# Spectral filter + GEGLU kernel: leftover columns in four groups of 32 partitions, twiddle tables split between VectorE and GpSimd, column loop written out

## The chip, the core and the metric

The kernel runs on one core of one Trainium2 chip. The metric is device time in microseconds (us) of one execution. TensorE is called PE (its weight loads PEld), VectorE DVE, ScalarE ACT, GpSimd POOL; SP is the engine whose instruction stream issues nearly all DMAs of this kernel, in program order.

## The reference

One transformer-like block on x of shape (1, 2048, 576), bf16: a spectral filter over the normalised x, then a GEGLU feed-forward network, each with a residual.

```python
def _A_ref(x, w_r, w_i):            # x: (1, 2048, 576); w_r, w_i: (2048, 289)
    X = rfft2(x.astype(float32), axes=(-2, -1))
    X = X * (w_r + 1j * w_i)
    return irfft2(X, s=(2048, 576), axes=(-2, -1)).astype(bfloat16)

def _B_ref(x, w_gate, w_up, w_down):   # w_gate, w_up: (576, 4608); w_down: (4608, 576)
    return (gelu(x @ w_gate) * (x @ w_up)) @ w_down

h   = x + _A_ref(layernorm(x), w_r, w_i)
out = h + _B_ref(layernorm(h), w_gate, w_up, w_down)
```

## The kernel before

The 2048 rows are split as 128 partitions times 16 (`h`), and the length-2048 Fourier transform as 16 (rows h, with a 128-wide table `F16`) and 128 (columns, with the twiddle tables). All is one program with `manual_schedule`: each engine executes its instructions in the order in which the program issues them, and so does each engine's DMA queue; engines meet through semaphores, which come from the data dependences and from the rotation of buffers. PSUM has four buffers of two banks (`two`), which all stages take in turn.

The stages, in order:

1. **Row stage** (about 4 to 21 us). x is loaded in six chunks. DVE (`sd`) and ACT (`ln_act`) make means and variances, POOL the reciprocal deviations (`ln_rstd`) and minus twice the means (`minus_means`). `norms(lo, hi)`: DVE scales the table `F16` by rstd of a row h into `FR`, and `row16(h)` multiplies on PE the columns of that row with it into PSUM (`f2t`), for the columns 0 to 255 and 288 to 543 of the 576. `evict` copies two rows at a time to `Bt[:, 0:4]` on ACT. The columns left over, 256 to 287 and 544 to 575, are the "leftovers" or "rests": `rests(h)` does four rows, each with four matmuls (`row16_rest`, L351) into 64 partitions for either half, and `evict4` copies them to `Bt[:, 4]`.
2. **Tables.** `DT` holds the sines and cosines of the column transform (`phases`, `col_sin`, `mirror`); `DF` is a copy of its third part for the leftovers' partitions, zero elsewhere. `DQ` is `DT` in another layout, made by small DMAs (`load_dq`). `TF` holds nine twiddles, each with minus sine, cosine and sine (slots 0, 1, 2); their angles are made on DVE (`angle_a` multiply-add, `angle_b` modulo 2048, `angle_s` shift, `angle_c` magnitude), the sines on ACT (`sine`, `cosine`), the negation on DVE (`minus_sine`). `first` are twiddles 0 and 1, `rest` are 2 to 8. `TI` is `TF` transposed by DMA from SP (`turn_tf`).
3. **Filter.** `WR` and `WI` hold rows 0 to 16 of the filter per partition: rows 0 to 8 come straight from HBM, rows 9 to 16 in reversed partition order, gathered by POOL into `wm` (`gather`) and copied from there by SP (L504). POOL then halves the first and the last column of all rows (L508).
4. **Column loop.** For the eight k of `order = [1, ..., 7, 0]`: `f2(c)` for c = k and k + 8 multiplies `Bt` with `DT` and `DF` on PE into `pq_ps` (six matmuls each, L550), `f2_out` copies to `pq`; `f3(k, half)` applies the twiddle (L567, L568; copies g and hs on ACT); `sum_of` combines the halves on DVE; `wmul` multiplies with the filter on DVE (`times`, L618, with rows k and 17 - k of WR, then of WI; `parts`, L623 and L624; Zt, L638 and L639 or, for k = 0, L641 and L642); `i3(k, s)` goes back with `TI` on PE (L658; for k = 0 L682), ACT copies to `EO`. Steps of neighbouring k are interleaved, `wmul` one and `i3` three iterations behind `f2`. `inv_cols` (L709) and `add_rows` then finish the inverse transform.
5. **FFN** (from about 65 us to the end). Layernorm, `gate` (L978, gate and up), the product with w_down (L1021, L1040), and the output.

Of the kernel before, what the change touches and what calls it, by code (L numbers as in the profile page):

```python
# [20 lines left out]
P = 128  # L21
# [21 lines left out]
def kernel_body(  # L43
# [45 lines left out]
    neg = keep.tile([P, 2], FP32, name="neg")  # L89
    for i in range(2):  # L90
        V.memset(neg[:, i : i + 1], -2.0 + i)
    mneg = keep.tile([P, 2, H], BF16, name="mneg")
# [18 lines left out]
    DF = keep.tile([P, 2, 2, JH], BF16, name="DF")  # L111
# [28 lines left out]
    def minus_means(lo, hi):  # L140
        sh = [P, 2, hi - lo]
        G.tensor_tensor(
            mneg[:, :, lo:hi],
            mv[:, lo:hi, 0].unsqueeze(1).to_broadcast(sh),
            neg[:].unsqueeze(2).to_broadcast(sh),
            ALU.mult,
        )
# [19 lines left out]
    for t, w in ((WR, A_w_r), (WI, A_w_i)):  # L167
        nc.sync.dma_start(t[:, 0:9, 0:J], w.rearrange("(p r) j -> p r j", r=H)[:, 0:9, :])
# [19 lines left out]
    V.memset(DF[:], 0.0)  # L188
# [18 lines left out]
    iota(iD[64:128, 2:3], [[0, 1]], 2 * P + 64 + 192, 1)  # L207
# [50 lines left out]
    first, rest = slice(0, 2), slice(2, 9)  # L258
# [15 lines left out]
    def angle_c(sl):  # L274
        drop_sign(ab[:, sl], ab[:, sl])

# [36 lines left out]
    def fill(dst, n):  # L313

        for _ in range(n):
            T.matmul(dst, lhsT=ident[:], rhs=h_sb[:, 0, 0:512], start=True, stop=True)

    def row16(h):
# [6 lines left out]
        for t in range(2):  # L325
            for n, d0 in ((0, t * P), (1, DH + t * P)):
# [9 lines left out]
                lhsT=mneg[:, 0, h : h + 1].to_broadcast([P, P]),  # L336
# [5 lines left out]
    def rests(h):  # L342
        ps_f["f4", h] = two("f4")
        for i in range(4):
            row16_rest(h + i)

    def row16_rest(h):
        o = (h % 4) * P
        for mean in (False, True):
            for p0, d0 in ((0, 256), (64, 512)):  # L350
                T.matmul(  # L351
                    ps_f["f4", h - h % 4][p0 : p0 + 64, 0, o : o + P],
                    lhsT=mneg[:, 1, h : h + 1].to_broadcast([P, 64]) if mean else h_sb[:, h, d0 : d0 + 64],
                    rhs=FR[:, h, 0, :],
                    start=not mean,
                    stop=mean,
                )
# [8 lines left out]
    def evict4(h):  # L366
        (V.tensor_copy if h >= 8 else A.copy)(
            Bt[:, 4, :].rearrange("p (c h l) -> p h c l", c=16, h=16)[:, h : h + 4, :, :],
            ps_f["f4", h][:, 0].rearrange("p (h c l) -> p h c l", h=4, c=16),
        )  # L370
# [71 lines left out]
    sd(2, 4)  # L442
# [19 lines left out]
    rests(0)  # L462
# [5 lines left out]
    rests(4)  # L468
# [4 lines left out]
    evict(0, 2)  # L473
    evict4(0)
    evict(4, 6)
    evict4(4)
# [6 lines left out]
    rests(8)  # L483
# [8 lines left out]
    rests(12)  # L492
# [5 lines left out]
    mirror(0)  # L498
    evict4(8)
    V.tensor_copy(DF[0:32], D3[0:32])  # L500
    V.tensor_copy(DF[96:128], D3[96:128])
    evict4(12)
    for w, t in ((WR, wm[0]), (WI, wm[1])):
        nc.sync.dma_start(w[:, 9 : H + 1, 0:J], t[:].rearrange("p (r j) -> p r j", r=8))  # L504
    angle_a(rest)
    angle_b(rest)
# [5 lines left out]
    def load_dq(r):  # L512
        for w in range(1 - r, NW):
            j0, j1 = w * JW, (w + 1) * JW
            for lo, hi in ((j0, min(j1, (j0 // P + 1) * P)), ((j0 // P + 1) * P, j1)):
                if lo < hi:
# [3 lines left out]
                    )  # L520

# [21 lines left out]
    def f2(c):  # L543
        ps = two("pq_ps")
        col = slice(slot[c] * P, (slot[c] + 1) * P)
        steps = [(par, t) for par in range(2) for t in (par, par + 2, 4)]
        if c == order[0]:
            steps.sort(key=lambda s: s[1] == 4)
        for par, t in steps:
            T.matmul(  # L550
                ps[:, par, 0:JP],
                lhsT=Bt[:, t, col],
                rhs=DT[:, t // 2, par] if t < 4 else DF[:, par],
                start=(t == par),
                stop=(t == 4),
            )
        pq[c] = wk.tile([P, 2, JP], BF16, name="pq", tag="pq", bufs=6)
        pq_ps[c] = ps
# [541 lines left out]
```

## Time and profile before

| | |
|---|---|
| Median of three timed runs | 494.39 us (494.04 to 494.93) |
| Profiled execution, its own time | 494.6 us |
| its span | 492.8 us, 12868 instructions |
| PE busy | 484.7 us (98%), PEld 338.9 (69%) |
| DVE busy | 223.4 us (45%) |
| ACT busy | 158.2 us (32%) |
| POOL busy | 29.5 us (6%) |
| Granted TensorE clock | 9 tenths or more in all 40 slices |

A line of the timeline has start and duration in us, engine, line, operation, output and inputs with their shapes, the number of instructions merged into it, and in brackets how long the engine had been idle and what ended the idle time. "SPq" is the issue of a DMA by SP; its data land later. A line of the table by stretches has the stretch, its length, then busy time and number of instructions of PE, PEld, DVE, ACT and POOL, the granted clock, the DMA share and GB/s. A line of the chain in order of time has start, duration, engine, tile and line. The duration of a DVE, ACT or PE instruction includes a tail that overlaps the next one; the cost of one in a row of them is the distance from start to start.

### The profile page before, as it was taken

What the parts mean: (1) busy time and instruction counts of PE and PEld (TensorE: products, weight loads), DVE (VectorE), ACT (ScalarE), POOL (GpSimd) and SP (SyncE); (2) the same over time, 40 slices, a digit from 0 to 9 for tenths busy, and PEclk for the clock granted to TensorE, in tenths of its full rate; (3) what the DMA queues carried; (4) which work ended last, traced back from release to release, by engine and by line L of the source; (5) the groups of instructions that cost most, each with busy time, mean ns of one, the idle gap of its engine ahead of it and who ended that gap; (6) DMA issues with size and microseconds to landing.
All of it is one profiled execution on the core that took longest, in us unless ns stands there. A gap on an engine that the chain in (4) does not pass through costs nothing.

```text
span 492.8 us, 12868 instructions
## 1 busy us (share of the span) xinstructions
PE 484.7 (98%) x5762; PEld 338.9 (69%) x5762; DVE 223.4 (45%) x457; ACT 158.2 (32%) x280; POOL 29.5 (6%) x84
## 2 busy tenths in 40 slices
PE   6999999999999999999999999999999999999997
PEld 3777789875589955555699755555799655555995
DVE  8999774798622177333311345333121333333111
ACT  8899863322210022332200132332110232232000
POOL 8500010011100011000000000000000000000000
PEclk9999999999999999999999999999999999999999
DMA  8838979769970049966720089876600377760000
GB/s 278 234 74 184 246 115 240 165 128 212 223 161 3 3 118 195 192 145 147 152 65 1 37 170 199 174 145 147 143 3 3 92 158 155 150 146 1 14 13 25
DMA packets 89582, 62.35 MB, mean 127 GB/s; under 512 B 23222, under 2 KB 88118, under 8 KB 89526
## 3 DMA queue, kind: packets, MB, share of 16 engines
q1 hardware_dynamic: 89238, 60.34, 57.5%
q0 software_dynamic: 288, 1.18, 0.7%
q8 instruction: 45, 0.74, 0.7%
q14 instruction: 11, 0.09, 0.1%
HBM read 52.65 MB, written 2.36 MB: 112 GB/s over the span
## 4 chain that ended last, share of the span: by engine, by line
PE 95%; ACT 2%; POOL 1%; DMA 1%; issue 0%; DVE 0%; ACTq 0%; POOLq 0%
PE gu L978 57%; PE acc L1021 27%; PE pq_ps L550 2%; PE cs_ps L709 2%; PE acc L1040 2%; PE eo_ps L658 2%; ACT junk L128 1%; PE y_ps L848 1%; PE gh_ps L568 1%; PE gh_ps L567 1%; DMA h_sb<-in_A_x_dram 1%; POOL rstd L138 1%; ACT Bt L361 0%; POOL wm_r L397 0%; PE eo_ps L682 0%
## 5 line engine op out<-in xcount | busy, mean ns | idle before, releaser
L978 PE MATMUL gu<-Bt,wgu 64*128 64x512 bf16 (+1 forms) x2646 | 270.6, 363 | 0.0
L978 PEld LDWEIGHTS <-wgu 64*128 64x128 bf16 x2646 | 151.5, 94 | 115.6 <-issue 0.3
L987 DVE TENSOR_TENSOR P_sb<-g_sb,gu 128x512 bf16<-128x512 f32 (+1 forms) x156 | 100.4, 645 | 140.3 <-ACT g_sb L986 140.3
L986 ACT ACTIVATE g_sb<-gu 128x512 f32<-128x512 f32 (+1 forms) x156 | 88.0, 564 | 193.5 <-PE gu L978 193.5
L1021 PEld LDWEIGHTS <-P_sb 64*128 64x128 bf16 x2160 | 122.2, 94 | 10.9
L1021 PE MATMUL acc<-wd,P_sb 64*128 64x288 bf16 x1440 | 90.9, 283 | 0.0
L1030 DVE TENSOR_TENSOR part<-part,acc 128x576 f32<-128x576 f32 x15 | 11.3, 754 | 112.6 <-ACT part L1029 112.6
L1029 ACT COPY part<-acc 128x576 f32<-128x576 f32 x15 | 9.6, 639 | 122.8 <-PE acc L1021 122.8
L1021 PE MATMUL acc<-wd_a,P_sb 64*128 64x288 bf16 x720 | 46.8, 283 | 0.0
L550 PE MATMUL pq_ps<-DT,Bt 128*128 128x290 bf16 x64 | 12.3, 286 | 0.7 <-ACT Bt L361 0.7
L978 PE MATMUL gu<-Bt,wgu_e 64*128 64x256 bf16 (+1 forms) x162 | 12.5, 305 | 0.0
L873 DVE TENSOR_SCALAR hrow<-h_sb,mv,rstd 128x1152 bf16<-128x1152 bf16 x14 | 12.2, 868 | 0.6 <-POOL rstd L911 0.6
L138 POOL TENSOR_TENSOR rstd<-rstd,mhalf 128x1 f32<-128x1 f32 (+2 forms) x17 | 12.0, 709 | 1.4
L1032 DVE TENSOR_TENSOR h_sb<-h_sb,part 128x576 bf16<-128x576 bf16 x15 | 11.4, 758 | 0.5
L550 PEld LDWEIGHTS <-Bt 128*128 128x128 bf16 x96 | 9.1, 97 | 3.4 <-ACT Bt L361 0.8
L978 PEld LDWEIGHTS <-wgu_e 64*128 64x128 bf16 x162 | 10.3, 94 | 1.2
L137 POOL TENSOR_SCALAR rstd<-mv 128x1 f32<-128x1 f32 (+2 forms) x17 | 4.1, 242 | 116.7 <-DVE mv L123 116.0
L561 ACT CAST pq<-pq_ps 128x580 bf16<-128x580 f32 x16 | 10.5, 666 | 1.2 <-PE pq_ps L550 1.1
L709 PE MATMUL cs_ps<-DQ,EO 58*128 58x290 bf16 x144 | 10.8, 283 | 0.0
L327 PE MATMUL f2t<-FR,h_sb 128*128 128x256 bf16 x64 | 9.2, 273 | 0.6 <-DVE FR L391 0.6
L709 PEld LDWEIGHTS <-EO 58*128 58x128 bf16 x160 | 7.8, 94 | 2.4 <-issue 0.7
L550 PE MATMUL pq_ps<-DF,Bt 128*128 128x290 bf16 x32 | 8.9, 285 | 0.0
(149 smaller groups left out, 283.9 us busy)
## 6 DMA issues: line engine op xcount, KB each, us to landing
wgu<-in_B_w_gate_dram SPq DMA_DIRECT2D x46, 432.0 KB, 5.1
wgu<-in_B_w_up_dram SPq DMA_DIRECT2D x46, 432.0 KB, 6.1
wd_a<-in_B_w_down_dram SPq DMA_DIRECT2D x1, 1728.0 KB
wd<-in_B_w_down_dram SPq DMA_DIRECT2D x1, 1728.0 KB
wd<-in_B_w_down_dram SPq DMA_DIRECT2D x6, 288.0 KB, 7.9
out_dram<-h_sb SPq DMA_DIRECT2D x3, 576.0 KB
h_sb<-in_A_x_dram SPq DMA_DIRECT2D x4, 288.0 KB, 4.3
h_sb<-in_A_x_dram SPq DMA_DIRECT2D x2, 576.0 KB
```

What stands on the lines that cost most here:

```text
L138: G.tensor_tensor(dst[:, sl], dst[:, sl], mhalf[:, sl], ALU.pow)
L550: T.matmul(ps[:, par, 0:JP], lhsT=Bt[:, t, col], rhs=DT[:, t // 2, par] if t < 4 else DF[:, par], start=(t == par), stop=(t == 4),)
L561: copy(pq[c][:, rs].rearrange("p r (j a) -> p r j a", a=2), pq_ps[c][:, :, 0:JP].rearrange("p a (r j) -> p r j a", r=2)[:, rs],)
L658: T.matmul(pv[:, n], lhsT=z[:, a, w].rearrange("p b j -> p (b j)"), rhs=TI[:, ts[k], 1 - a : 3 - a, :], start=(a == 0), stop=(a == 1),)
L709: T.matmul(ps[:, e, 0:JP], lhsT=EO[x][rows, w, 2 * g : 2 * g + 2].rearrange("p h e k l -> p (h e k l)"), rhs=DQ[rows, w] if w or e else DT ...
L873: V.tensor_scalar(hrow[:], h_sb[:, h, :].rearrange("p (r k) -> p r k", k=64).unsqueeze(2).to_broadcast([P, NR, 2, 64]), mv2[:, h, 0:1], rs ...
L978: T.matmul(gu[:, c, 0:n], lhsT=w[rows, r, i * P : (i + 1) * P], rhs=hl[tcnk % 2][rows, r, lo:hi], start=(r == 0), stop=(r == NR - 1),)
L986: A.activation(g_sb, gu[:, 0, 0:n], ACT.Gelu_apprx_tanh)
L987: V.tensor_tensor(p_sb(f)[:, lo:hi], g_sb, gu[:, 1, 0:n], ALU.mult)
L1021: T.matmul(accs[i][:, c, 0:DH], lhsT=p_sb(f)[rows, st * P : (st + 1) * P], rhs=wd[f // NWA][rows, f % NWA, c * DH : (c + 1) * DH], start=( ...
L1030: V.tensor_tensor(part, part, accs[1][:, :, 0:DH], ALU.add)
L1032: V.tensor_tensor(hv, hv, part, ALU.add)
```

## The change

The leftover columns of a row pair k, k + 8 are laid out in four groups of 32 partitions. `rests` does eight rows with ten matmuls each into 32 partitions and 64 columns; `evict4` is called twice instead of four times. In `f2` the pair is done together: eight full matmuls, then four with 32 rows of `Bt` and of `D3` each, without `DF`. The twiddles are split in `part_a` (2 to 4, angles on DVE as before) and `part_b` (5 to 8, angles on POOL, `pool_angles`). The first two pairs' second column copies go to DVE. The column loop is written out, with `f2` of two pairs ahead of the first `f3`. `load_filter` stands later, and `turn_tf(part_a)` stands ahead of the copies from `wm`. The diff, cut to its core:

```diff
@@ -138,13 +135,7 @@ minus_means
-        G.tensor_tensor(mneg[:, :, lo:hi], ..., neg[:]..., ALU.mult)
+        G.tensor_scalar(mneg[:, lo:hi], mv[:, lo:hi, 0], -2.0, None, op0=ALU.mult)
@@ -164,8 +155,11 @@
-    for t, w in ((WR, A_w_r), (WI, A_w_i)):
-        nc.sync.dma_start(t[:, 0:9, 0:J], w.rearrange("(p r) j -> p r j", r=H)[:, 0:9, :])
+
+    def load_filter():
+        V.memset(WR[:, 0, 0:2], 0.0)
+        for t, w in ((WR, A_w_r), (WI, A_w_i)):
+            nc.sync.dma_start(t[:, 0:9, 0:J], w.rearrange("(p r) j -> p r j", r=H)[:, 0:9, :])
@@ -185,7 +179,8 @@
-    V.memset(DF[:], 0.0)
+    for t, b in ((edge[:, 0, 0], hpib), (edge[:, 0, 1], nhpib), (edge[:, 1]..., zerob)):
+        A.activation(t, zerob[0:2].to_broadcast(list(t.shape)), ACT.Sin, bias=b[0:2])
@@ -274,6 +270,24 @@
+    def pool_angles(sl):
+        v, t = pr[:, sl].bitcast(FP32), ab[:, sl]
+        for k in range(sl.start, sl.stop):
+            G.tensor_scalar(
+                pr[:, k].bitcast(FP32), q16[:], s2p[:, 0:1], ks[:, k : k + 1], op0=ALU.mult, op1=ALU.add
+            )
+        G.tensor_scalar(t, v, 1.0 / S, C23, op0=ALU.mult, op1=ALU.add)
+        G.tensor_scalar(t, t, -C23, -float(S), op0=ALU.add, op1=ALU.mult)
+        G.tensor_tensor(v, v, t, ALU.add)
+        G.tensor_scalar(t, v, 0.0, 2.0, op0=ALU.max, op1=ALU.mult)
+        G.tensor_tensor(t, t, v, ALU.subtract)
+
+    def sine_signed(sl):
+        A.activation(TF[:, sl, 2, :], pr[:, sl].bitcast(FP32), ACT.Sin, bias=zerob[:], scale=2.0 * PI / S)
+
+    def cosine_signed(sl):
+        A.activation(TF[:, sl, 1, :], ab[:, sl], ACT.Sin, bias=hpib[:], scale=-2.0 * PI / S)
@@ -333,28 +347,30 @@
-    def rests(h):
...
+    def rests(h0):
+        ps = ps_f["f4", h0] = two("f4")
+        for h in range(h0, h0 + 8):
+            o = (h - h0) * 64
+            F = FR[:, h].rearrange("p s (x e n) -> p s x e n", x=2, e=2)
+            for n in range(3):
+                for e in range(2):
+                    for par in range(1 if n == 2 else 2):
+                        p0 = 64 * e + 32 * par
+                        T.matmul(
+                            ps[p0 : p0 + 32, 0, o : o + 64],
+                            lhsT=mneg[:, h : h + 1].to_broadcast([P, 32])
+                            if n == 2
+                            else h_sb[:, h, 256 + DH * n : 288 + DH * n],
+                            rhs=F[:, par if n == 1 else 0, :, e],
+                            start=(n == 0),
+                            stop=(n == 2 - par),
+                        )
@@ -439,7 +455,9 @@
     minus_row()
-    sd(2, 4)
+    sd(2)
+    load_filter()
+    sd(4)
@@ -489,21 +503,26 @@
     norms(14, 16)
-    rests(12)
+    rests(8)
     evict(8, 10)
     col_sin(1, pd, zerob)
     col_sin(0, kd, hpib)
     evict(12, 14)
     mirror(1)
     mirror(0)
+    part_a, part_b = slice(2, 5), slice(5, 9)
+    pool_angles(part_b)
+    angle_a(part_a)
+    angle_b(part_a)
+    sine(part_a)
     evict4(8)
-    V.tensor_copy(DF[0:32], D3[0:32])
-    V.tensor_copy(DF[96:128], D3[96:128])
-    evict4(12)
+    angle_s(part_a)
+    angle_c(part_a)
+    minus_sine(part_a)
+    cosine(part_a)
+    turn_tf(part_a)
     for w, t in ((WR, wm[0]), (WI, wm[1])):
         nc.sync.dma_start(w[:, 9 : H + 1, 0:J], t[:].rearrange("p (r j) -> p r j", r=8))
-    angle_a(rest)
-    angle_b(rest)
     for w in (WR, WI):
         G.tensor_scalar(w[:, :, 0 : J : J - 1], w[:, :, 0 : J : J - 1], 0.5, None, op0=ALU.mult)
@@ -540,22 +561,34 @@
-    def f2(c):
...
+    def f2(k):
+        cc = (k, k + 8)
+        for c in cc:
+            ps = pq_ps[c] = two("pq_ps")
+            if c == order[0]:
+                for _ in range(32):
+                    T.matmul(ps[0:32, 0, 0:16], lhsT=ident[:, 0:32], rhs=h_sb[:, 0, 0:16], start=True, stop=True)
+            for par in range(2):
+                for t in (par, par + 2):
+                    T.matmul(
+                        ps[:, par, 0:JP],
+                        lhsT=Bt[:, t, slot[c] * P : (slot[c] + 1) * P],
+                        rhs=DT[:, t // 2, par],
+                        start=(t == par),
+                        stop=False,
+                    )
+            pq[c] = wk.tile([P, 2, JP], BF16, name="pq", tag="pq", bufs=6)
+        for e, c in enumerate(cc):
+            col = (slot[c] // 8 * 4 + slot[c] % 4) * P
+            for par in range(2):
+                rows = slice(64 * e + 32 * par, 64 * e + 32 * par + 32)
+                T.matmul(pq_ps[c][:, par, 0:JP], lhsT=Bt[rows, 4, col : col + P],
+                         rhs=D3[rows, par], start=False, stop=True)
@@ -629,14 +659,18 @@ wmul
+            if i == 1:
+                minus_sine(part_b)
+                sum_of(nxt, 0)
+                sum_of(nxt, 1)
@@ -735,56 +769,56 @@
-    for i in range(n + 1):
...
+    o = order
+    f2(o[0])
+    f2_out(o[0])
+    f2_out(o[0] + 8, V.tensor_copy)
+    f2(o[1])
+    f2_out(o[1])
+    f2_out(o[1] + 8, V.tensor_copy)
+    f3(o[0], 0)
+    f3(o[0], 1)
+    sum_of(o[0], 0)
+    sum_of(o[0], 1)
+    f3(o[1], 0)
+    f3(o[1], 1)
+    sine_signed(part_b)
+    f2(o[2])
+    both_out(o[2])
+    cosine_signed(part_b)
+    f2(o[3])
+    both_out(o[3])
+    wmul(o[0], 1, o[1])
+    turn_tf(part_b)
+    f3(o[2], 0)
+    f3(o[2], 1)
+    load_dq(0)
+    pre = [load_gu(g) for g in range(3)]
+    nc.sync.dma_start(wd_a[:], wd_view[:, 0:NWA, :])
...
+    for s in range(3):
+        i3(o[0], s)
+    wmul(o[1], 2, o[2])
+    for j in range(3, 8):
+        f3(o[j], 0)
+        f3(o[j], 1)
+        if j < 7:
+            f2(o[j + 1])
+            both_out(o[j + 1])
+        else:
             inv_cols(0, 0)
             inv_cols(0, 1)
+        for s in range(3):
+            i3(o[j - 2], s)
+        wmul(o[j - 1], j, o[j])
+    wmul(o[7], 8)
+    V.tensor_scalar(G16v[1], G16v[0], -1.0, None, op0=ALU.mult)
```

(`both_out(k)` is `f2_out` of k and of k + 8 on ACT.)

More of the change, by code (lines that the diff above doesn't have):

```diff
@@ L88, in kernel_body @@
     V.memset(mhalf[:], -0.5)
[L89 to L92, printed above, removed]
+    mneg = keep.tile([P, H], BF16, name="mneg")
     Bt = keep.tile([P, NDT, S], BF16, name="Bt")
@@ new lines, in kernel_body @@
+    f3(o[2], 1)
+    load_dq(0)
+    pre = [load_gu(g) for g in range(3)]
+    nc.sync.dma_start(wd_a[:], wd_view[:, 0:NWA, :])
+    scr_pool.__exit__(None, None, None)
+    eop = ctx.enter_context(tc.tile_pool(name="eop", bufs=1, side="right"))
+    EO = [eop.tile([P, 5, H, 2, 4, 8], BF16, name=f"EO{x}", tag=f"EO{x}") for x in range(2)]
+    for s in range(3):
[8 more added lines that the diff above has]
+        else:
```

129 lines of the change are left out of this document (27 added, 102 removed).

## The prediction

> **What bounds the kernel now.** The span is 492.8 us, the profiled execution took 494.6, and the three timed runs have a median of 494.39 (494.04 to 494.93), so the execution lies 0.2 above the median and sums made in it can be carried to the median unchanged. A measurement of this kernel can tell about 0.2%, 1.0 us, from no change. I read the chain that ended last first, then the busy time by stretches, then the timeline of the stretch the diff touches (10 to 56 us).
>
> ```profile
> PE 95%; ACT 2%; POOL 1%; DMA 1%; issue 0%; DVE 0%; ACTq 0%; POOLq 0%
> ...
> 30.00:40.00 10.00, 9.94 (x85) 7.98 (x84) 10.00 (x24) 9.77 (x18) 0.00 (x0) 1.00 0.48 88
> 40.00:50.00 10.00, 10.00 (x95) 7.84 (x93) 10.00 (x24) 9.82 (x18) 0.00 (x0) 1.00 1.09 229
> ...
> 36.33 0.74 PE pq_ps L550 x6
> ...
> 38.06 0.74 PE pq_ps L550 x6
> 38.80 1.09 PE eo_ps L658 x10
> 39.89 0.74 PE pq_ps L550 x6
> ```
>
> The columns of a stretch are PE, PEld, DVE, ACT and POOL. The chain names PE, but from 30 to 50 us DVE is busy for all of it and ACT for 9.8 of 10. One step of the column loop (one twiddle k) costs PE 39.89 - 36.33 = 3.56 us: twelve matmuls of `f2` at 0.74 for six, 1.48 together; eight of `f3`, 38.06 - 36.33 - 0.74 = 0.99; ten of `i3`, 1.09. DVE's step is one `wmul`:
>
> ```profile
> 27.49 0.77 DVE L618 TENSOR_TENSOR m<-xab,WR 128x1156 bf16<-128x1156 bf16 x1
> 28.17 0.76 DVE L618 TENSOR_TENSOR m<-xab,WI 128x1156 bf16<-128x1156 bf16 x1
> ...
> 31.07 0.76 DVE L618 TENSOR_TENSOR m<-xab,WR 128x1156 bf16<-128x1156 bf16 x1
> ...
> 34.64 0.76 DVE L618 TENSOR_TENSOR m<-xab,WR 128x1156 bf16<-128x1156 bf16 x1
> ...
> 51.71 0.45 DVE L639 TENSOR_TENSOR Zt<-zb,za 128x580 bf16<-128x580 bf16 x1
> ...
> 52.47 1.27 PE L658 MATMUL eo_ps<-TI,Zt 128*128 128x256 bf16 x10
> ...
> 53.99 0.46 DVE L642 TENSOR_TENSOR Zt<-m,m 128x580 bf16<-128x580 bf16 x1
> ...
> 55.02 1.31 PE L682 MATMUL eo_ps<-TI,Zt 128*64 128x128 bf16 x40
> ```
>
> From one first product to the next DVE takes 34.64 - 31.07 = 3.57 us, without a pause, so both engines run at their own rate and happen to agree. They meet where `i3` reads Zt: the seventh Zt is written at 51.71 + 0.45 = 52.16 and PE takes it up at 52.47; the last at 54.45, and PE at 55.02. So PE has no more than 0.3 us of slack over DVE in the loop. Whatever PE saves beyond this, it would spend waiting for DVE; whatever DVE is late beyond it, the end is late. The question for this change is therefore when DVE's string of eight `wmul` can start, and what lies in it.
>
> **The change part by part.** *Leftovers in f2.* Per pair (k, k+8), four full matmuls go, and four of 32 rows come in. A full one takes 0.74 / 6 = 0.123. A change of tile shape has a price in the old leftover pass:
>
> ```profile
> 15.27 0.22 PE L351 MATMUL f<-FR,h_sb 128*64 128x128 bf16 x2
> 15.33 0.22 PE L351 MATMUL f<-FR,mneg 128*64 128x128 bf16 x2
> 15.48 0.28 PE L327 MATMUL f2t<-FR,h_sb 128*128 128x256 bf16 x1
> ```
>
> 128 columns stream in 15.33 - 15.27 = 0.06 a pair of half-width tiles (x2: two start together), but 15.48 - 15.33 = 0.15 pass where the shape changes back to full: 0.09 more, which I take for each change. If the four run side by side, a pair costs 8 x 0.123 + 0.123 + 2 x 0.09 = 1.29 instead of 1.48: 0.19 saved, 1.5 us in eight. If they run one behind another it is 1.66, 1.4 us lost in eight. The trace has halves side by side and no quarters; I take side by side, nearest to these rows. Either way it is PE's time, and the slack above says that at most 0.3 us of a saving is seen.
>
> *Leftovers in the first stage.* Per eight rows, 80 matmuls of 64 columns in four column groups replace 32 of 128 in two. Three rounds of four per row, at 0.03 to 0.06 a round, give 0.7 to 1.4 us; only two at a time, five rounds, 2.2. I take 1.0, and two changes of shape. [...] The two tiles that start together inside one 0.06 speak for a cost that is shared; no row here has a moving side under 128 columns.
>
> The first 80 come while rows 8 to 11 are awaited; the second 80 come behind row 15. The end of the evictions then stays:
>
> ```profile
> 18.86 0.22 POOL L142 TENSOR_TENSOR mneg<-mv,neg 128x4 bf16<-128x4 f32 x1
> ...
> 19.98 1.93 ACT L361 CAST Bt<-f2t 128x1024 bf16<-128x1024 f32 x2
> ...
> 20.50 0.22 PE L334 MATMUL f2t<-FR,mneg 128*128 128x128 bf16 x1
> ...
> 21.96 0.30 PE L550 MATMUL pq_ps<-DT,Bt 128*128 128x290 bf16 x1 [0.68 <-ACT Bt L361]
> ```
>
> Row 15 is on PE until 20.56 because the last rstd comes from POOL (to 19.08), and ACT's last eviction ends at 19.98 + 1.93 = 21.91, ahead of which `f2` cannot start (21.96). The one eviction fewer on ACT falls into its waits for rows 9 and 11. The second leftovers end at 20.56 + 0.1 + 1.0 = 21.65, the 32 small filling matmuls behind them between 21.75 and 23.7 (nothing to 0.06 each): `f2` starts up to 1.7 late. That is covered by what follows.
>
> *The tables, and what SP is made to wait for.* This is the part that decides. `turn_tf(part_a)` now stands on SP's queue ahead of the two copies that bring rows 9 to 16 of WR and WI from wm, which `wmul` of k=1 needs (it reads rows 1 and 16, after POOL has halved both ends). Before:
>
> ```profile
> 10.51 1.43 SPq L287 DMA_TRANSPOSE TI<-TF  x1
> 16.70 0.74 SPq L504 DMA_DIRECT2D WR<-wm_r  x1
> 20.11 0.61 SPq L504 DMA_DIRECT2D WI<-wm_i  x1
> ...
> 22.01 0.41 POOL L508 TENSOR_SCALAR WR<-WR 128x34 bf16<-128x34 bf16 x1 [2.92 <-DMA WR<-wm_r]
> ...
> 24.09 0.48 POOL L508 TENSOR_SCALAR WI<-WI 128x34 bf16<-128x34 bf16 x1 [1.30 <-DMA WI<-wm_i]
> ```
>
> The copies were issued as soon as the gathers had landed (16.70, 20.11), landed 5.3 and 4.0 us later (POOL's waits end at 22.01 and 24.09), and were ready long before the product at 27.49. Now they wait for the sines of twiddles 2 to 4:
>
> ```profile
> 20.54 0.68 DVE L367 CAST Bt<-f 128x512 bf16<-128x512 f32 x1
> 21.13 0.29 DVE L500 COPY DF<-DT 32x580 bf16<-32x580 bf16 x1
> ...
> 22.50 1.15 DVE L245 SCALAR_TENSOR_TENSOR pr<-q,s2p,ks 128x896 int32<-128x896 f32 x1
> 23.68 0.63 DVE L269 TENSOR_SCALAR pr<-pr 128x896 int32<-128x896 int32 x1
> 24.34 0.73 DVE L272 TENSOR_SCALAR ab<-pr 128x896 f32<-128x896 int32 x1
> 25.11 0.63 DVE L232 TENSOR_SCALAR ab<-ab 128x896 int32<-128x896 int32 x1
> 25.66 0.42 DVE L284 TENSOR_SCALAR TF<-TF 128x896 bf16<-128x896 bf16 x1
> ...
> 28.69 0.41 ACT L281 ACTIVATE TF<-ab,nhpib 128x128 bf16<-128x128 f32 x1
> ...
> 29.52 0.95 ACT L281 ACTIVATE TF<-ab,nhpib 128x768 bf16<-128x768 f32 x1
> ```
>
> Those are seven twiddles; three take 3/7, with start to start as the cost. DVE is free of the mirrors at 20.54. Angles: 1.18 x 3/7 = 0.51, 0.66 x 3/7 = 0.28, to 21.33. The leftovers' eviction waits for PE (21.65 + 0.1), takes 21.13 - 20.54 = 0.59: 22.35. The shifted angle 0.33 and its magnitude 0.24: 22.92. Then ACT's cosine, 384 wide, between 0.41 (128) and 0.95 (768), 0.63: 23.55; its sine went in at 21.91, and DVE's negation hides beside the cosine. SP issues the transposition at 23.6, 1.43 as for the first (two twiddles): 25.0. WR follows at 25.0, WI at 25.75. WI took 4.0 us to land with nothing but WR ahead of it and 2.1 behind WR (24.09 - 22.01): WR at 29.0, WI at 31.1. Bounds: 29.75 if WI doesn't queue behind WR, 32.4 if WR takes 5.3 again. POOL halves WI in 0.48: the second product can start at 31.6 instead of 28.17.
>
> POOL's own new work does not hold this: four multiply-adds and five passes of 512 columns, from 19.1.
>
> ```profile
> 3.74 0.89 POOL L256 TENSOR_SCALAR pr<-q,s2p,ks 128x128 int32<-128x128 f32 x2
> ...
> 5.94 0.57 POOL L264 TENSOR_SCALAR kd<-kd 128x438 f32<-128x438 f32 x1
> ```
>
> 4 x 0.45 plus 5 x 0.6 (438 columns took 0.57), twice that for the two-input passes: 4.8 to 6.0, done by 25.1, four microseconds before WR lands. Were that cover gone, POOL would have held the halving itself.
>
> *The string after it.* Behind the second product the step's remainder is as before, 31.07 - 28.17 = 2.90; the negation of four twiddles now lies in it, 0.33 x 4/7 = 0.19. So the second `wmul` starts at 31.6 + 2.90 + 0.19 = 34.7 instead of 31.07: 3.6 late. All further `wmul` are unchanged and DVE has no pause to give back. Less the 0.3 of slack, PE reads the last two Zt 3.3 us late, and everything behind (row transforms, FFN) is PE's own rate: **+3.3**. What is saved on PE, the one product sum read from bf16 instead of PSUM, the G16 negation (now behind the last `wmul`), the two column copies on DVE and the later `f2` all lie ahead of the wait that ends at 31.6 or in PE's idle time beside it.
>
> Nothing comes from the rest: the late load of the filter's first nine rows is wanted only with the halving; `minus_means` on POOL is one small instruction as before; the `edge` sines run before the first x lands. Forecast: 494.39 + 3.3 = **497.7 us**.
>
> **The rivals.** *A, faster: PE is the bound and its saving comes through.* For it: the chain runs 95% over PE. Then 1.5 saved, less about 0.4 for fillers: 493.3. It decides if WI is halved before 28.17 and DVE gets through a step in less than PE's new 3.37. Against: DVE's 10.00 of 10 and start-to-start of 3.57 with no wait. *B, no change: the copies are in time.* SP would have to take them ahead of the transposition, or land them in two microseconds less. Then the first product waits for `f2` of two pairs (2.6 from 21.96), `f3` (1.0), ACT's copy of its second half and two sums:
>
> ```profile
> 28.16 0.65 ACT L589 CAST hs<-gh_ps 128x578 bf16<-128x578 f32 x1
> ...
> 28.84 0.46 DVE L600 TENSOR_TENSOR xab<-g,hs 128x578 bf16<-128x578 bf16 x1
> 29.22 0.46 DVE L623 TENSOR_TENSOR za<-m,m 128x580 bf16<-128x580 bf16 x1
> ```
>
> 21.96 + 2.6 + 1.0 + 0.65 + 2 x 0.38 = 27.0, with 0.06 to 0.1 for each of five handovers 27.4, where it was 27.49, and up to 1.2 more if the fillers delay `f2`, of which I allow 0.4; 0.2 for the negation, 0.3 of slack: 494.2 to 494.9. *C, the four row groups run one behind another.* 1.66 a pair makes PE's step 3.74, over DVE's 3.57: 0.17 in each of five steps behind the wait, 0.9 on top of the forecast, 498.6; without the wait, 495.8. *D, the wait is longer:* second leftovers at 2.2 and a slow WR, 1.2 + 1.3 more: 500.2.
>
> **How the numbers follow.** The forecast 0.64, C 0.08, D 0.05: slower 0.77. A 0.11. B 0.12. The forecast's own range is WI from 29.75 to 32.4, so +1.9 to +4.6: 496.3 to 499.0. Taking in B below and C above, the range is 494.3 to 499.2; left out are A, D and the edges. Faster by over 0.2% 0.11, within 0.12, slower 0.77.
>
> **What would show it.** Right: SP issues WR's copy behind a transposition at 23 to 25 us; DVE idle for two to four microseconds ahead of its first or second product, released by POOL's halving of WR or WI; PE idle around 31 to 34 with Zt as releaser; steps of 3.57 behind it; `f2` pairs of about 1.3 with four starts together. Wrong: the copies issued before 21 us, the first product at 27.5, or steps shorter than 3.5 on DVE. A gap on PE ahead of `i3` without one on DVE would mean that another engine, ACT, holds the loop.

## The result and the profile after

| | before | after |
|---|---|---|
| Median | 494.5 us (494.04 to 494.93, 6 runs) | 503.37 us (502.64 to 504.03, 6 runs) |
| Ratio after / before, 95% interval | | 1.0177 (1.0167 to 1.0188) |
| Profiled execution, its own time | 494.6 us | 504.03 us |
| its span | 492.8 us | 502.2 us |

The change costs 8.9 us; 497.7 was forecast, with a range up to 499.2. The sign and the place were right, the size was not. The six times of after lie around two values, 502.64 to 502.96 and 503.77 to 504.03, and the profiled execution is of the upper ones (five further runs of the same kernel, below, do not divide so clearly; more at the end).

The timeline of the changed kernel, first SP's queue:

```profile
26.32 1.30 SPq L301 DMA_TRANSPOSE TI<-TF  x1
27.71 0.75 SPq L525 DMA_DIRECT2D WR<-wm_r  x1
28.55 0.74 SPq L525 DMA_DIRECT2D WI<-wm_i  x1
```

The transposition of twiddles 2 to 4 stands ahead of WR and WI on SP, as the prediction said, but it is issued at 26.32, not 23.6. Then POOL, one of its two-input passes over the angles (L281) and the halving (L527):

```profile
22.53 1.64 POOL L281 TENSOR_TENSOR pr<-pr,ab 128x512 f32<-128x512 f32 x1
...
33.40 0.39 POOL L527 TENSOR_SCALAR WR<-WR 128x34 bf16<-128x34 bf16 x1 [5.80 <-DMA WR<-wm_r]
...
35.23 0.38 POOL L527 TENSOR_SCALAR WI<-WI 128x34 bf16<-128x34 bf16 x1 [1.07 <-DMA WI<-wm_i]
```

WR lands 33.40 - 27.71 = 5.7 us after its issue, WI 35.23 - 28.55 = 6.7 after its own. And DVE, from the mirrored tables (L436) to the second `wmul`:

```profile
20.90 1.62 DVE L436 TENSOR_SCALAR DT<-DT,sgn 128x216 bf16<-128x216 bf16 x4 [1.11 <-ACT DT L424]
...
23.08 1.31 DVE L265 TENSOR_SCALAR pr<-pr 128x384 int32<-128x384 int32 x1
...
33.82 0.77 DVE L648 TENSOR_TENSOR m<-xab,WR 128x1156 bf16<-128x1156 bf16 x1 [4.20 <-POOL WR L527]
35.65 0.77 DVE L648 TENSOR_TENSOR m<-xab,WI 128x1156 bf16<-128x1156 bf16 x1 [1.06 <-POOL m L550]
...
38.34 0.83 DVE L630 TENSOR_TENSOR xab<-g,hs 128x578 bf16<-128x578 bf16 x2
39.20 0.77 DVE L648 TENSOR_TENSOR m<-xab,WR 128x1156 bf16<-128x1156 bf16 x1
...
42.78 0.76 DVE L648 TENSOR_TENSOR m<-xab,WR 128x1156 bf16<-128x1156 bf16 x1
```

The two waits in brackets, 4.20 us for POOL's halving of WR and 1.06 behind that of WI, are of the kind that was forecast, only longer. The second `wmul` starts at 39.20, where it was 31.07: 8.1 late instead of 3.6. From there DVE's step is 42.78 - 39.20 = 3.58, unchanged. Last PE, its clock by stretches (the columns PE, PEld, DVE, ACT, POOL, then the granted clock), and the end of the loop, DVE's seventh Zt and PE's last two `i3`:

```profile
38.32 2.29 PE L692 MATMUL eo_ps<-TI,Zt 128*128 128x256 bf16 x10 [5.66 <-issue]
...
46.39 1.15 PE L573 MATMUL pq_ps<-DT,Bt 128*128 128x290 bf16 x8
47.47 0.30 PE L585 MATMUL pq_ps<-DT,Bt 32*128 32x290 bf16 x4
47.71 0.50 PE L692 MATMUL eo_ps<-TI,Zt 128*128 128x256 bf16 x3
```
```profile
30.00:40.00 10.00, 4.34 (x34) 2.74 (x34) 4.95 (x11) 4.32 (x8) 1.18 (x7) 0.82 0.47 120
40.00:50.00 10.00, 10.00 (x72) 6.83 (x71) 10.00 (x24) 8.23 (x14) 0.00 (x0) 0.83 0.58 120
```
```profile
59.91 0.46 DVE L669 TENSOR_TENSOR Zt<-zb,za 128x580 bf16<-128x580 bf16 x1
```
```profile
61.64 1.27 PE L692 MATMUL eo_ps<-TI,Zt 128*128 128x256 bf16 x10
...
64.19 1.31 PE L716 MATMUL eo_ps<-TI,Zt 128*64 128x128 bf16 x40
```

PE is idle from 32.7 to 38.3 (5.66 us in brackets; the profile names no releaser, but the Zt that `i3` reads is complete at 37.76 + 0.46 = 38.22). Behind that the ten matmuls of `i3` take 2.29 us where they take 1.27 at full clock (61.64); the clock, 1.00 in these stretches before, is 0.82 and 0.83. `i3` of the seventh column starts at 61.64, 1.27 behind its Zt (59.91 + 0.46), where it was 0.3 behind. `i3` of k = 0 starts at 64.19 instead of 55.02: 9.2 late, which is the whole of 504.03 - 494.6 = 9.4 but for 0.2.

### The profile page after: what moved, and what is told of

It reads as the page before. It is cut to its first block, busy times and chain, and to the rows that moved or that the text cites. A ratio compares the mean times of both kernels' runs of the same rounds, so it can differ in the third digit from the quotient of the medians.

```text
span 502.2 us, 13136 instructions
## 1 busy us (share of the span) xinstructions
PE 486.7 (97%) x5890; PEld 340.3 (68%) x5890; DVE 223.3 (44%) x455; ACT 158.7 (32%) x282; POOL 37.7 (8%) x95
## 4 chain that ended last, share of the span: by engine, by line
PE 93%; DVE 2%; DMA 2%; issue 1%; ACT 0%; SPq 0%; POOL 0%
PE gu L1012 56%; PE acc L1055 26%; PE cs_ps L743 2%; PE eo_ps L692 2%; PE acc L1074 2%; DMA WI<-wm_i 1%; PE y_ps L882 1%; PE pq_ps L573 1%; DMA h_sb<-in_A_x_dram 1%; PE f2t L341 1%; PE gh_ps L601 1%; PE gh_ps L600 1%; DVE st L400 0%; DVE st L402 0%; DVE DT L436 0%
## 5 line engine op out<-in xcount | busy, mean ns | idle before, releaser
L692 PE MATMUL eo_ps<-TI,Zt 128*128 128x256 bf16 x70 | 9.9, 294 | 5.7 <-issue 5.7
L692 PEld LDWEIGHTS <-Zt 128*128 128x128 bf16 x70 | 6.7, 104 | 8.0 <-issue 6.4
L573 PE MATMUL pq_ps<-DT,Bt 128*128 128x290 bf16 x64 | 9.7, 296 | 0.2 <-ACT Bt L377 0.2
L600 PE MATMUL gh_ps<-pq,TF 128*128 128x289 bf16 x32 | 9.1, 307 | 0.2 <-ACT pq L594 0.2
```

The lines of the kernel that those rows point to most:

```text
L573: T.matmul(ps[:, par, 0:JP], lhsT=Bt[:, t, slot[c] * P : (slot[c] + 1) * P], rhs=DT[:, t // 2, par], start=(t == par), stop=False,)
L600: T.matmul(dst, lhsT=TF[:, ts[k1], t0, :], rhs=a, start=True, stop=False)
L692: T.matmul(pv[:, n], lhsT=z[:, a, w].rearrange("p b j -> p (b j)"), rhs=TI[:, ts[k], 1 - a : 3 - a, :], start=(a == 0), stop=(a == 1),)
```

## The experiments

The kernel before ran beside each of them; its medians were 494.33 to 494.43.

**The order of the copies.** The two copies go ahead of the transposition on SP; nothing else differs from the changed kernel.

```diff
-    turn_tf(part_a)
     for w, t in ((WR, wm[0]), (WI, wm[1])):
         nc.sync.dma_start(w[:, 9 : H + 1, 0:J], ...)
+    turn_tf(part_a)
```

> The changed kernel with one thing undone: SP takes the two copies from wm (WR, WI rows 9 to 16) ahead of the transposition of part_a. Theory (the loss is the copies' place in SP's queue): the copies are issued near 16.7 and 20.1 us, POOL halves both right behind its angles (27.6 to 29.0), DVE's first product follows its sums at about 29.6 instead of 33.8 and its second wmul starts near 33.9 instead of 39.2; PE waits less than 1 us ahead of the first i3 and keeps its full clock; total about 497 us (495.5 to 498.5), against 503.4. Rival 1 (the loss comes from the row stage, the tables and DVE beside POOL, and the copies are hidden): 502 or more.

Measured: 496.56 us (496.35 to 496.78), 1.0044 of before (1.0029 to 1.006). Of 8.9 us the order of three DMAs holds 6.8. This kernel's profile is without the pause that is described at the end; against the lower of the two values of after (502.75 in the middle) the order holds 6.2.

```profile
16.34 0.75 SPq L524 DMA_DIRECT2D WR<-wm_r  x1
...
24.80 1.30 SPq L301 DMA_TRANSPOSE TI<-TF  x1
```
```profile
22.81 1.30 DVE L228 TENSOR_SCALAR ab<-ab 128x384 int32<-128x384 int32 x1
...
27.25 0.86 DVE L630 TENSOR_TENSOR xab<-g,hs 128x578 bf16<-128x578 bf16 x2 [1.18 <-ACT hs L619]
...
32.79 0.77 DVE L648 TENSOR_TENSOR m<-xab,WR 128x1156 bf16<-128x1156 bf16 x1
```

WR's copy is issued at 16.34, as before, and the transposition waits until 24.80 with nothing behind it that anybody needs soon. The second `wmul` is 1.7 late instead of 8.1. The row at 22.81 is taken up below, where POOL's part in the prediction is told.

**The delay alone.** In the kernel before, the copies and the halving go behind seven of the DQ copies on SP, and nothing else is changed.

```diff
-    for w, t in ((WR, wm[0]), (WI, wm[1])):      # copies, and POOL's halving
...
     load_dq(1)
+    for w, t in ((WR, wm[0]), (WI, wm[1])):
```

> The kernel before, with only the two copies from wm and POOL's halving moved behind the seven DQ copies in SP's queue. Theory: WR is issued near 26.8 us, WI is halved near 33 us, DVE's second wmul starts about 5 us late (36 instead of 31.1), and the end is as late plus up to 1.5 us for a halved TensorE clock after PE's wait: 499 to 501.5 us against 494.5. Rival 1: the copies are hidden, no change. Rival 2 (DVE's lateness is made good by PE or ACT within the loop): under 497.

Measured: 501.62 us (501.06 to 501.95), 1.0141 (1.0126 to 1.0157).

```profile
31.60 0.41 POOL L519 TENSOR_SCALAR WR<-WR 128x34 bf16<-128x34 bf16 x1 [12.64 <-DMA WR<-wm_r]
```
```profile
32.04 0.77 DVE L618 TENSOR_TENSOR m<-xab,WR 128x1156 bf16<-128x1156 bf16 x1 [4.73 <-POOL WR L519]
...
36.75 0.76 DVE L618 TENSOR_TENSOR m<-xab,WR 128x1156 bf16<-128x1156 bf16 x1
```

A kernel with none of the change but late copies is 7.3 us slower. Its second `wmul` starts 36.75 - 31.07 = 5.7 late, and the time grows by more than that: here, too, PE is idle for 5.68 us, the ten matmuls of its first `i3` take 2.29, and DVE then waits 0.88 for hs in the third `wmul` (42.63).

**The clock.** 24 matmuls on a tile that nobody reads are put ahead of the first `i3`, where PE is idle.

```diff
+    warm = two("warm")
+    fill(warm[:, 0, :], 24)             # matmuls of 512 columns
     for s in range(3):
         i3(o[0], s)
```

> The changed kernel with 24 matmuls of 512 columns on data of no use, into a PSUM buffer of their own, ahead of the first i3, where PE waited 5.7 us. At 0.215 us each they fill about 5.2 us of that wait. Theory: PE's clock stays full behind it, the first ten i3 matmuls take 1.1 instead of 2.3 us, and PE, which stood 1.25 us behind DVE's Zt all through the loop, stands 0.1 to 0.3 behind: total 0.9 to 1.3 us less (about 502.2). Rival A (the halved clock is hidden, since DVE sets the pace): no change. Rival B (the halved clock is most of the loss): 3 us less or more.

Measured: 501.47 us (501.36 to 501.67), 1.0143 of before (1.0127 to 1.0158), and 1.9 less than the changed kernel's median. Not all of that is the clock.

```profile
31.20 5.34 PE L330 MATMUL warm<-h_sb,ident 128*128 128x512 bf16 x24
36.94 1.25 PE L692 MATMUL eo_ps<-TI,Zt 128*128 128x256 bf16 x10 [0.40 <-issue]
...
41.62 1.25 PE L692 MATMUL eo_ps<-TI,Zt 128*128 128x256 bf16 x10 [1.12 <-DVE Zt L669]
```
```profile
37.82 0.77 DVE L648 TENSOR_TENSOR m<-xab,WR 128x1156 bf16<-128x1156 bf16 x1
```

The first `i3` takes 1.25, with the granted clock at 1.00 from 30 to 50 us, and from its second column on PE waits for DVE (41.62); the seventh `i3` starts 0.1 behind its Zt (59.01 against 58.46 + 0.46) instead of 1.27. That is the clock's part, 1.2. The second `wmul`, which the added matmuls don't touch, starts 39.20 - 37.82 = 1.4 earlier than in the profile of the changed kernel, because this execution has no pause. Against the lower value of after (502.75) the median gains 1.3. So useless work on PE saves some 1.3 us here.

**The pause in the leftovers' burst.** The first 80 leftover matmuls are issued as two times 40, the second 40 and their eviction behind row 9.

```diff
-    rests(0)
+    rests(0, 0, 4)                      # rows 0 to 3
...
-    evict4(0)
...
-    norms(8, 12)
+    norms(8, 10)
+    rests(0, 4, 8)
+    evict4(0)
+    norms(10, 12)
```

> The changed kernel with the first burst of 80 leftover matmuls cut in two of 40, the second behind rows 8 and 9. Theory (the burst outruns what feeds PE with instructions: 0.39 and 0.49 us of 'issue' in it and 1.2 us in all from 15.4 to 16.9): the gaps go, ACT's last eviction ends near 22.2 instead of 23.2, and the tables, the transposition, the copies and the end move with it: 0.8 to 1.2 us less, about 502.4. Rival: the leftovers cost the same wherever they stand (a price of each matmul): no change, row 15 ends at 21.3 as before.

Measured: 502.63 us (502.15 to 503.88). The pause is gone from its profile, but the interval overlaps that of the changed kernel, whose runs don't all have the pause: this experiment decides nothing by itself.

**POOL beside DVE.** The angles of twiddles 5 to 8 go back to DVE, into its wait for WR.

```diff
-    pool_angles(part_b)
...
     sum_of(o[0], 1)
+    angle_a(part_b); angle_b(part_b); angle_s(part_b); angle_c(part_b)
```

> Part B's angles are put back on DVE, behind the first column's sums, where DVE waited 4.2 us for the halved WR in the changed kernel; POOL does none of them. Theory (DVE beside a busy POOL is slow, and this holds the transposition up): the mirror falls from 1.62 to about 1.05 and the masking of part A's angles from 1.31 to about 0.3, the transposition is issued some 1.5 us earlier (24.7 instead of 26.3), so are the column copies behind it and the first product: about 501.9 us. Part B's own angle work on DVE (some 2.5 us) fits into the 4.2 us wait. Rival 1 (POOL costs DVE nothing that matters): 503.4, no change. Rival 2 (it does not fit into the wait and pushes the products): 504 or more.

Measured: 502.2 us (501.9 to 502.93), 1.0164 (1.015 to 1.0178); the control beside it 503.38.

```profile
23.56 1.30 SPq L301 DMA_TRANSPOSE TI<-TF  x1
24.95 0.75 SPq L524 DMA_DIRECT2D WR<-wm_r  x1
```
```profile
19.46 0.92 DVE L436 TENSOR_SCALAR DT<-DT,sgn 128x216 bf16<-128x216 bf16 x4
...
20.93 0.36 DVE L265 TENSOR_SCALAR pr<-pr 128x384 int32<-128x384 int32 x1
```
```profile
31.05 0.40 POOL L526 TENSOR_SCALAR WR<-WR 128x34 bf16<-128x34 bf16 x1 [11.98 <-DMA WR<-wm_r]
```

The transposition is issued at 23.56, where the prediction had 23.6, and the terms on the way agree as well (the leftovers' eviction at 21.53 for 21.75, the cosine at 22.92 for 22.92). The mirrors take 0.92 (1.62 beside POOL) and the masking 0.36 (1.31). Of the 2.76 us that it comes earlier, 20.90 - 19.46 = 1.44 are the mirrors' earlier start, on an execution without the pause; the other 1.3 are DVE at its own speed. The copies-first and the clock kernel confirm the split: their profiles have POOL's passes and no pause, and both issue the transposition at 24.80, 1.2 later than here. Little of it arrives: WR's copy flies longer, 31.05 - 24.95 = 6.1 us, WI's 33.21 - 25.79 = 7.4, and the second `wmul` starts at 37.18, only 0.6 earlier than in the clock kernel (37.82).

**PE's order in the loop.** `f2` of the next pair is put ahead of this column's `f3`.

```diff
-        f3(o[j], 0); f3(o[j], 1)
         if j < 7:
             f2(o[j + 1]); both_out(o[j + 1])
+        f3(o[j], 0); f3(o[j], 1)
```

> In the steady loop the next column pair's f2 is put ahead of this one's f3. Theory (PE fell 1.3 us behind DVE while its clock was halved, and can't catch up since f3's second matmul waits for ACT's copy of a pair that was only just finished, which holds PE's step at 3.57): the step of PE falls to about 3.4, its lag behind the last Zt write shrinks from 1.25 to 0.3 or less by the last column, and the time is some 0.9 us lower, about 502.5. Rival (the lag's 1.25 us is not what sets the end, or ACT's rate holds PE): no change, 503.4.

Measured: 503.84 us (503.13 to 504.4): no gain.

```profile
61.46 0.72 PE L692 MATMUL eo_ps<-TI,Zt 128*128 128x256 bf16 x5
```
```profile
45.13 0.47 DVE L630 TENSOR_TENSOR xab<-g,hs 128x578 bf16<-128x578 bf16 x1 [1.04 <-ACT hs L619]
...
60.93 0.46 DVE L669 TENSOR_TENSOR Zt<-zb,za 128x580 bf16<-128x580 bf16 x1
```

The lag of `i3` behind the seventh Zt is 61.46 - 61.39 = 0.1, but not because PE caught up: its `i3` starts 0.2 earlier than in the changed kernel (61.64), while the Zt is complete 1.0 later (61.39 instead of 60.37). DVE now waits 1.04 us for hs (45.13), since `f3` stands behind the slow `f2` (its first eight matmuls take 2.14 us, and 1.15 from the next pair on). In both orders what PE lost at half clock reaches the end, by PE in one and by DVE in the other.

**The control.**

> The changed kernel itself, as the control for the other runs of this call and to see whether its runs fall into two groups (some 503.8 with a pause of about a microsecond in the burst of leftover matmuls, some 502.7 without). Theory: both appear, median 502.7 to 503.9. Rival (the pause belonged to that one profiled execution): all within 0.3 us of one value, and the profile shows no pause with the same time.

Measured: 503.38 us (501.87 to 504.11). The five times are 501.87, 503.07, 503.38 and twice 504.11: neither two groups nor one value, so neither the theory nor the rival holds as it was put. The profiled execution has the pause and 504.11.

**Copies first, halving between POOL's passes.**

```diff
+    for w, t in ((WR, wm[0]), (WI, wm[1])): ...   # ahead of pool_angles
     pool_angles(part_b)                # now halves WR and WI behind its first sum
...
+    cosine(part_a); turn_tf(part_a)    # behind the first two columns' f2_out
```

> The copies go ahead of the transposition, as in the swapped kernel; POOL halves the columns between its passes over the angles (behind the first sum, once they have landed) instead of behind the last pass; and part A's cosine and transposition go behind the first two columns' evictions on ACT. Theory (what remained of the loss in the swapped kernel, 496.6, were POOL's late halving and ACT's cosine in front of the first eviction): the first product starts at about 27.4 instead of 28.2 and the second follows at once, 0.8 to 1.1 us gained: about 495.6. Rival 1 (the sums bound the products, and they wait for f3): 496.4. Rival 2 (leftovers and shared evictions bring their own gain besides): 494 or less.

Measured: 497.4 us (496.98 to 498.11), 1.0065 (1.0051 to 1.0079): 0.8 more than copies first alone.

```profile
23.09 1.36 DVE L303 TENSOR_SCALAR TF<-TF 128x384 bf16<-128x384 bf16 x1
...
27.20 0.84 DVE L630 TENSOR_TENSOR xab<-g,hs 128x578 bf16<-128x578 bf16 x2 [1.41 <-ACT hs L619]
...
28.80 1.83 DVE L648 TENSOR_TENSOR m<-xab,WI 128x1156 bf16<-128x1156 bf16 x1
```
```profile
28.63 1.38 POOL L288 TENSOR_TENSOR ab<-ab,pr 128x512 f32<-128x512 f32 x1
```

The second product takes 1.83 instead of 0.77 beside POOL's last two-input pass, and the negation of three twiddles (23.09) 1.36 where that of seven took 0.42 before. The first sum waits for hs as it did. The earlier halving lets the second product start at 28.80 instead of 29.24, but its 1.83 us take back more than that: the second `wmul` starts at 33.42, in the copies-first kernel at 32.79.

**Each part alone.** Three kernels: the leftovers' part with the changed loop (but the first columns' copies back on ACT, and `f3` of the first ahead of the copies of the second) and all angles on DVE; the same with the loop of the kernel before; and the angle part alone in the kernel before, copies first.

```diff
# leftovers alone, on the changed kernel        # angles alone, on the kernel before
-    pool_angles(part_b)                        +    pool_angles(part_b)
-    angle_a(part_a); angle_b(part_a); ...      -    angle_a(rest); angle_b(rest)
+    rest = slice(2, 9)                         +    angle_a(part_a); angle_b(part_a)
+    angle_a(rest); angle_b(rest)
```

> The leftovers' part alone: the changed kernel with the angles, sines and cosines of columns 2 to 8 all on DVE and ACT, in the kernel before's order and behind the column copies, POOL without angle work, and the early column copies of f2 on ACT only. Theory (the whole loss belongs to the angle part, which put a transposition ahead of the column copies and POOL's passes beside DVE): first product at 27.5 to 28.5, second wmul at 31 to 32, TensorE's clock full throughout: 493.5 to 495.3. Rival (the four groups of 32 or the pairing of k and k+8 cost something by themselves, through the later evictions on ACT or the lost direct read of gh_ps): 496 or more.

> The leftovers' part alone again, but with the kernel before's loop: f3 of a column ahead of the next column's evictions, the first sum reading gh_ps directly, the sums interleaved from the first wmul on; f2 still does k and k+8 together. Theory (of the 3.2 us of the first leftovers kernel some 1.6 came from the loop's order, where DVE waited 1.21 us for hs in the second wmul and the sums stood behind the first one): second wmul at 31.5 to 32.5, steps of 3.57 from there: 495.0 to 496.0. Rival A (all of it is the burst of 80 leftover matmuls and its pause, ahead of ACT's evictions): 497 to 498. Rival B (the pairing saves PE time that now counts): 494.4 or less.

> The angle part alone, with nothing put ahead of the copies: the kernel before with its leftovers, its column order and its evictions, but the angles of columns 5 to 8 on POOL, the halving between POOL's passes, and both transpositions where they were, behind the copies. Theory (parts add up: the changed kernel with the copies ahead is 2.2 us slower than before and the leftovers' part alone 3.2 us, so the angle part takes off about 1.0): 493.4. Rival 1 (it takes off nothing, since the first sum waits for f3 and not for the angles, and the products run beside POOL's passes, where one took 1.83 us instead of 0.77): 494.4 to 495.5. Rival 2: 496 or more, if POOL's passes slow DVE's angles of columns 2 to 4 as in the changed kernel.

Measured: 497.58 us (496.69 to 498.37), 1.006 (1.0046 to 1.0074); with the loop of before 495.53 (495.44 to 496.66), 1.0024 (1.0013 to 1.0034); angles alone 495.83 (495.47 to 498.03), 1.0031 (1.0011 to 1.0052).

```profile
35.35 0.47 DVE L624 TENSOR_TENSOR xab<-g,hs 128x578 bf16<-128x578 bf16 x1 [1.21 <-ACT hs L613]
```
```profile
22.65 0.69 DVE L383 CAST Bt<-f 128x512 bf16<-128x512 f32 x1 [0.80 <-PE f L365]
...
32.98 0.76 DVE L645 TENSOR_TENSOR m<-xab,WR 128x1156 bf16<-128x1156 bf16 x1
```
```profile
21.43 0.70 DVE L527 COPY DF<-DT 32x580 bf16<-32x580 bf16 x1
...
23.61 0.42 PE L572 MATMUL pq_ps<-DF,Bt 128*128 128x290 bf16 x2 [0.71 <-DVE Bt L390]
...
26.75 1.43 DVE L622 TENSOR_TENSOR xab<-g,gh_ps 128x578 bf16<-128x578 bf16 x2 [0.29 <-ACT g L611]
...
28.34 0.75 DVE L640 TENSOR_TENSOR m<-xab,WR 128x1156 bf16<-128x1156 bf16 x1
```

My theory that all of the loss lies in the angle part fell with the first of them: in its loop DVE waits 1.21 us for hs in the second `wmul` (35.35), a wait that the loop of before does not have. With that loop the leftovers cost 1.1 in the median. Its profiled execution is the slowest of eight (496.66), and it is late from the start: its first rows are scaled at 10.51, those of the kernel before at 9.47. The second `wmul` starts at 32.98, 1.9 late; of the 0.9 that are left, DVE's eviction, which waits 0.80 for PE (22.65), is the part that can be seen. The angles cost 1.4 with the copies where they were, with a wide interval. Beside POOL each DF copy takes 0.70 instead of 0.29, so the last leftovers' eviction is late, PE waits 0.71 for it in the first `f2` (23.61), and the first sum and product follow late: 28.34 instead of 27.49, although four sevenths of the angles were taken off DVE. (The three twiddles' multiply-add takes 1.15 us beside POOL, as long as that of all seven did before.) That 1.1 + 1.4 is near the 2.2 us of the copies-first kernel does not show that the parts add up: that kernel has the changed loop, with which the leftovers alone cost 3.2. Neither part gains anything, and no kernel tried beats the one before.

**DQ's packets.** The eight DQ copies go behind the second transposition.

```diff
-    load_dq(1)
...
     turn_tf(part_b)
+    load_dq(1)
```

> In the changed kernel the eight DQ copies (32.9 KB and less each) go behind the second transposition on SP, so that none of their 290-byte packets stands beside WR's and WI's. Theory A (the copies' flight of 5.65 and 6.6 us is long because they share the queue with DQ's packets): they land at 4.0 to 5.4 us after the issue, the first product starts 0.5 to 1 us earlier: about 502.5. Theory B (it is the transposition's packets ahead of them and their own 2 x 578 KB side by side, at some 300 GB/s): the flight stays, 503.4.

Measured: 504.16 us (504.0 to 505.14).

```profile
27.50 0.75 SPq L525 DMA_DIRECT2D WR<-wm_r  x1
```
```profile
33.18 0.39 POOL L527 TENSOR_SCALAR WR<-WR 128x34 bf16<-128x34 bf16 x1 [5.81 <-DMA WR<-wm_r]
```

WR's flight is 5.7 us, as with DQ behind it: theory A fails. That does not show theory B. In the late kernel the copies have no transposition ahead of them, only DQ copies, and fly as long, 31.60 - 25.44 = 6.2 us for WR and 33.43 - 26.24 = 7.2 for WI.

## Why the prediction was right and wrong

Right were the cause and, in kind, its signs: SP takes WR and WI behind a transposition that waits for sines, DVE is idle ahead of both products, released by POOL's halving, and the loss is the delay of a string of `wmul` that has no pause to give back. The copies-first kernel shows that it is the order (6.2 to 6.8 of 8.9), the late kernel that late copies suffice. But WR's copy is issued at 27.71 instead of 23 to 25, DVE waits 4.20 and 1.06 us instead of two to four, and PE's wait is 32.7 to 38.3 instead of 31 to 34. Right, too, were DVE's step (3.58) and the pair of `f2`: 47.71 - 46.39 = 1.32 (forecast 1.29), with the four row groups side by side, 47.71 - 47.47 = 0.24 for all four with the change of shape. So rivals A and C had no ground.

What failed are sizes: four terms of the sum were too small, and one, what PE's wait does to its clock, was put at nothing. In the profiled execution `i3` of k = 0 is 9.2 late instead of 3.3. The missing 5.9 by step:

| step of the prediction | forecast | measured | difference |
|---|---|---|---|
| SP issues the transposition | 23.6 | 26.32 | 2.7 |
| WI's copy issued | 25.75 | 28.55 | 0.1 more |
| WI lands after its issue | 5.35 | 6.7 | 1.3 |
| second product to second `wmul` | 3.1 | 39.20 - 35.65 = 3.55 | 0.45 |
| PE behind DVE at the end of the loop | none | 1.27 | 1.3 |

Together 5.85.

*The transposition.* This is the largest miss, 2.7, and it has two parts. "POOL's own new work does not hold this" is the step that failed: it makes 1.2 to 1.3 of the 2.7. I priced POOL's passes by POOL's time, 4.8 to 6.0 us (they took 8.4, from 19.18 to 27.60: the one-input ones of 512 columns 0.62, 0.63 and 1.99, the two-input ones 1.64 and 1.27), and called them hidden. The sum was right in itself (without POOL's passes the issue is at 23.56) but DVE's work beside them is not at its own price: the masking at 23.08 takes 1.31 where 0.28 was reckoned and ends just behind POOL's two-input pass (22.53 to 24.17). In the copies-first kernel it is the magnitude that is slow, 1.30 (22.81) instead of 0.36, and it, too, ends just behind that pass of POOL (22.49 to 23.90). The other 1.5 (26.32 against 24.80 there) go with the pause described at the end, which the profile before did not show. Beside a two-input pass of POOL the traces also show the negation of three twiddles, one input in SBUF, at 1.36 (23.09 in the kernel that halves between POOL's passes; 0.28 in the changed kernel) and a product of two SBUF tensors at 1.83 (28.80 there) instead of 0.77, while two sums that read one input from PSUM took 1.43 beside such a pass (26.75 in the angles-alone kernel) and 1.41 in the kernel before, where POOL was idle:

```profile
25.99 1.41 DVE L600 TENSOR_TENSOR xab<-g,gh_ps 128x578 bf16<-128x578 bf16 x2
```

What slows DVE beside POOL no row shows. The prediction had no term for it.

*The flight.* I took 4.0 for a copy by itself from the row before, and one queue place for the second. There the copies were issued 3.4 us apart; here 0.84, behind a transposition. Neither is shown to be the reason: the late kernel's copies fly 6.2 and 7.2 without a transposition ahead, and in the kernel that halves between POOL's passes WI, issued 3.5 us after WR, flies 26.32 - 20.10 = 6.2. The flights shown here go from 4.0 us (WI in the kernel before) to 7.4; what sets them stays open.

*The second `wmul`.* The changed `wmul` no longer has the next column's sums inside the first step but behind it (38.34, 0.83 for two). This stood in the diff, and I carried 2.90 over from the old order.

*PE.* The prediction had PE idle at 31 to 34 and called that free; what idle time does to the clock was not priced. The wait became 5.66 us, and in the trace PE's lag behind it is 1.27. The kernel that keeps PE busy gains 1.9 us on the median, of which some 1.3 are the clock. PE does not make up for it by the end of the loop, and in the reordered kernel, where the lag is gone, DVE waits instead.

*The cover of the later `f2`.* "The end of the evictions then stays" was wrong for some executions: in the profiled one ACT's last eviction ended at 21.32 + 1.91 = 23.23, not at 21.91, and the mirrors, which wait for ACT, started the later:

```profile
21.32 1.91 ACT L377 CAST Bt<-f2t 128x1024 bf16<-128x1024 f32 x2
```

Rival B's price falls as well: with the copies in time it was to be 494.2 to 494.9, and it is 496.6, because the sums start at 27.25, the second product (29.24) waits for POOL's late halving, and the next column's sums stand behind the first `wmul`. The nearest was D, 500.2, which lengthened the wait alone; its 2.2 us for the second leftovers was an estimate that no run shows (0.7, at the end).

## What to carry to other kernels

An instruction on an in-order DMA queue costs what is queued behind it (6.2 to 6.8 of 8.9 us here): before moving one ahead of others, find the time at which its input is ready, and who needs the next. Work moved to POOL is not free for being off the path: add to the sum what DVE's instructions beside it become. Here the masking of three twiddles took 0.36 us without POOL, 0.42 and 0.66 beside one-input passes (21.16 in the kernel that halves between POOL's passes, 21.26 in the copies-first kernel) and 1.31 beside a two-input one (23.08 in the changed kernel). And where a change makes TensorE wait for several microseconds, look at the clock behind the wait: after waits of 4.67 to 5.68 us the ten matmuls of `i3` took 2.29 us here, after 0.78 and 1.12 us (copies first) 1.25.

## What the runs showed of the hardware

- PE idle for 5.66 us was followed by matmuls at half rate for several microseconds (ten of `i3` in 2.29 us, 1.27 at the end of the loop), with 0.82 and 0.83 as the mean granted clock of two stretches of 10 us: together 3.5 us of lost clock, or some 7 at half. By stretches of 1 us the clock is 0.74 from 36 to 37, then 0.50, and 0.84 from 43 to 44: it falls to half at some 36.5, 3.8 us after PE stopped, and is full again at some 43.3, 5.0 after the first `i3`; in the late kernel, reckoned from its mean clocks of 0.71 (30 to 40) and 0.95 (40 to 50), these are 2.9 and 4.0, and the half clock lasts 6.8 in both. With the angles back on DVE a wait of 4.67 us was followed by the same 2.29; in the copies-first kernel, where PE waits 0.78 (31.91) and 1.12 us (36.60) ahead of `i3`, the clock is 1.00 from 20 to 60 us and the ten take 1.25 both times.
- 80 leftover matmuls of 64 columns in four column groups (first row of the second burst):

```profile
21.38 0.24 PE L365 MATMUL f<-FR,h_sb 128*32 128x64 bf16 x8
```

  From 21.38 to 22.09, where the next matmuls start, that is 0.7 us, 9 ns each. The prediction's 1.0 us for them was an estimate.
- In the first burst PE stopped twice in some executions, with no releaser in the profile:

```profile
15.99 0.23 PE L365 MATMUL f<-FR,h_sb 128*32 128x64 bf16 x3 [0.39 <-issue]
16.71 0.23 PE L365 MATMUL f<-FR,h_sb 128*32 128x64 bf16 x4 [0.49 <-issue]
```

  That is a pause of some 1.1 us, in the profiles of the changed kernel, its control, the reordered, the DQ-late and the first leftovers kernel, and not in those of the copies-first kernel, the clock kernel, the one with the angles back on DVE, the one that halves between POOL's passes and the second leftovers kernel, which have the same burst. The two values of the changed kernel, some 1.1 apart, would fit it, but the control's five times do not divide so, and both profiled executions of the changed kernel have the pause; what stops PE there stays open.
